# A hand-ordered beginning with raw weights ahead, in a two-layer kernel behind linear attention

## The chip, the cores and the metric

The kernel runs on one core of a Trainium2 chip. The metric is the device time of one execution in microseconds (us); lower is better. The engines are TensorE (PE, matrix multiplications), VectorE (DVE), ScalarE (ACT), GpSimd (POOL) and SyncE (SP, which here only starts transfers). Transfers (DMA) are started by an engine's queue and moved by 16 DMA engines.

## The reference

Linear attention on 8 batches of 8 heads, 576 tokens and head size 64, then two layers on the 4608 tokens of 512 features:

```python
kv  = np.einsum('bhsd,bhse->bhde', k, v)
out = np.einsum('bhsd,bhde->bhse', q, kv)
rms = np.sqrt(np.mean(out * out, axis=-1, keepdims=True) + 1e-06)
x   = (out / rms * g_norm)            # transposed to 4608 x 512
h   = x @ w_in;  x = (h * np.cos(h)) @ w_out        # 512 x 2048, 2048 x 512
a, b = x @ w1, x @ w2;  out = ((a * b) @ w3) @ w_out2
```

## The kernel before

All products are made in three matmuls: each fp32 operand is split in a rounded part (hi, ACT by line 113) and the rest (lo, DVE or POOL by line 115), and hi·hi, hi·lo and lo·hi are summed in PSUM (L532 to L534).

**Attention.** A unit u is half a batch (288 tokens); there are 16. Heads go in four pairs p. For a batch, `emit_kv` sums kᵀv of a pair (20 matmuls, L272) and `evac_kv` splits it; for a unit, `emit_qs` splits q, `emit_out` makes q·kv (3 matmuls, L313 to L315), `evac_out` squares it on ACT, `emit_ms` makes the mean squares (L332). Then comes the norm: `emit_rs` copies the mean squares (`ms_sb`) to DRAM and back in another shape (transfers `msd`, `rsx`), `emit_newton` finds the inverse root with 11 small DVE operations (L367 and L352 to L358), `emit_bc` sends it through DRAM once more (`rsd`) and spreads it over partitions (`bc`), `emit_x` multiplies, and `split_x` makes x in two parts. Units 2 and 3 use POOL's queue for all of these transfers (`queue`), the others SP's. Units 0 and 1 have a way of their own, `first_units`: their norm never leaves the chip (mean squares by L421, 11 operations of 96x48, spread over partitions by matmuls of L435).

**First layer.** A step n is a token block t of 512 tokens and a block m of 128 of the 2048 hidden features: `emit_h` (12 matmuls, h), `g_first` and `g_rest` (ACT and DVE: u, the cosine, then `u<-u,h` by L558, which also frees h's PSUM, and the split into g by L115), and two steps later `emit_w` (12 matmuls of g with w_out into x2). Steps 0 to 7 are t=0, m=0 to 7; steps 8 to 23 are t=1; then the rest. Token block 0 needs units 0 and 1, block 1 needs units 1 to 3.

**Weights.** w_in and w_out arrive as float64 words in 32 chunks of 512 KB (i0, i1 … of w_in, u0, u1 … of w_out), which `convert` turns into fp32 (one ACT operation and four on DVE, L142, L143, L146, L149) and `put` splits (ACT and DVE). Eight chunks are asked for, converted and put behind the first units ahead of step 0, the others among the steps.

**What sets the order.** The program is written in the order above, and the build's scheduler then places every instruction on its engine by a model of times of its own. The order is fixed when the program is built; on the chip an engine takes its instructions in that order and waits for what is not there yet. `issue_after(i)` holds what is written under it behind instruction i in that schedule. `marks[0]` is a small POOL operation (the gate) behind the second square of the third pair, and the loads of units 2 and 3 stand behind it. `quick` says at which step n which stage of units 2 and 3 is written.

Of the kernel before, what the change touches and what calls it, by code (L numbers as in the profile page):

```python
# [7 lines left out]
F32 = mybir.dt.float32  # L8
# [5 lines left out]
P = 128  # L14
# [15 lines left out]
def f32(ap):  # L30
    return ap.bitcast(F32)
# [3 lines left out]
def kernel(  # L35
# [75 lines left out]
    def split(dst, src, lo_engine=None):  # L111

        nc.scalar.activation(dst[:, 0], src, AF.Copy)  # L113
        lo_engine = lo_engine or even(src.shape[-1])
        lo_engine.tensor_tensor(dst[:, 1], src, f32(dst[:, 0]), ALU.subtract)  # L115
# [234 lines left out]
    def newton(x, y, t):  # L350

        nc.vector.tensor_scalar(  # L352
            y.bitcast(I32), x.bitcast(I32), -0.5, RSQRT_SEED, ALU.mult, ALU.add
        )
        for _ in range(3):
            nc.vector.tensor_tensor(t, x, y, ALU.mult)
            nc.vector.scalar_tensor_tensor(t, t, 0.5, y, ALU.mult, ALU.mult)
            nc.vector.scalar_tensor_tensor(y, t, 1.5, y, ALU.subtract, ALU.mult)  # L358
# [33 lines left out]
    def first_units(spread):  # L392

        for p in range(NPAIR):
            emit_kv(0, p)
            evac_kv(0, p)
            for u in range(2):
                if p == 0:
                    o_sb[u] = ap.tile([P, NPAIR, HALF], F32, tag="osb", bufs=3, name=f"o_{u}")
                hl = ap.tile([P, 2, HALF], F32R, tag="hl", bufs=2, name=f"qhl_{u}_{p}")  # L400
                split(hl, q_raw.pop((u, p)), nc.vector)
                ps = ps_acc.tile([P, 512], F32, tag=f"acc{(2 * p + u) % 4}", name=f"out_{u}_{p}")
                o, w = ps[:, 0:HALF], kv_sb[p]
                nc.tensor.matmul(o, w[:, 0], hl[:, 0], start=True, stop=False)
                nc.tensor.matmul(o, w[:, 1], hl[:, 0], start=False, stop=False)
                nc.tensor.matmul(o, w[:, 0], hl[:, 1], start=False, stop=True)
                sq = ap.tile([P, HALF], F32, tag="tmp", bufs=5, name=f"sq_{u}_{p}")
                nc.scalar.activation(sq, o, AF.Square)
                nc.scalar.activation(o_sb[u][:, p, :], o, AF.Identity, scale=gneg)
                if p == NPAIR - 2 and u == 1:  # L410
# [6 lines left out]
                if p == 0 and u == 0:  # L417
                    mst = ps_h.tile([P, 512], F32, tag="h", name="ms_first")
# [6 lines left out]
        n = 4 * NPAIR * NT3  # L425
        x, y, t = (row(f"rs_first_{i}")[0:T3, 0:n] for i in range(3))
        nc.vector.tensor_scalar(x, mst[0:T3, 0:n], EPS, HUGE, ALU.add, ALU.min)
        newton(x, y, t)
        for u in range(2):
            for p in range(NPAIR):  # L430
                ps = ps_acc.tile([P, 512], F32, tag=f"acc{p}", name=f"spread_{u}_{p}")
                for k in range(NT3):
                    at = ((u * NT3 + k) * NPAIR + p) * 2
                    for h in range(2):
                        nc.tensor.matmul(  # L435
                            ps[D * h:D * h + D, T3 * k:T3 * k + T3],
                            y[:, at + h:at + h + 1].to_broadcast([T3, D]), spread[0:T3],
                            start=k == 0, stop=True, skip_group_check=True,
                        )
                o = o_sb[u][:, p, :]  # L440
                nc.vector.tensor_tensor(o, o, ps[:, 0:HALF], ALU.mult)

    NEWTON, LAST = 8, 10
# [67 lines left out]

    def split_x(t, c, units=None):
# [8 lines left out]
        while done < TB:  # L521
            u, s = divmod(t * TB + done, HALF)
            w = min(TB - done, HALF - s)
            if units is None or u in units:
                split(
# [336 lines left out]
    if True:  # L862
# [8 lines left out]
        spread = wpool.tile([P, T3], F32, tag=f"wi{NM - 1}", name="spread")  # L871
# [4 lines left out]
        )  # L876

# [5 lines left out]
        load_kv(0, 0, "wi0")  # L883
        load_rest(0)
        for p in range(1, NPAIR):
            load_kv(0, p, f"wi{p}")
        for h in range(2):
            nc.sync.dma_start(
                out=gneg[D * h:D * h + D], in_=g_norm.rearrange("(d o) -> d o", o=1)
            )  # L890
        nc.vector.tensor_scalar(gneg, gneg, -1.0, None, ALU.mult)
        for p in range(NPAIR):
            for u in range(2):
                load_q(u, p, f"wi{4 + 2 * p + u}")
        first_units(spread)
        for c in range(KD):
            split_x(0, c)
        for _ in range(4):
# [22 lines left out]
        for n in range(NS + 2):  # L921
# [228 lines left out]
```

## Time and profile before

| | |
|---|---|
| runs before (us) | 1537.47, 1538.57, 1538.18; median 1538.18 |
| span of the profiled execution | 1537.0 us |
| the runs' median over that span | 1.2 us |
| PE busy | 1493.1 us, 97% of the span |
| DVE, ACT, POOL busy | 60%, 45%, 24% |
| granted PE clock in 40 slices of 38.4 us | 0.7 in the first, 0.9 or more in all others |

The page gives the profiled execution by its span alone, so that the sum of a change is made on the span of 1537.0 us and compared with the runs by the 1.2 us that their median stands above it. A row of the timeline reads: start in us, length in us, engine, line, operation, out<-in, shapes, count, and in brackets the idle time of the engine ahead of it with what ended that. The length of a matmul counts its way through the pipeline; matmuls that follow each other closely start 0.23 us apart at full clock and 0.43 us apart at half clock.

### The profile page before, as it was taken

What the parts mean: (1) busy time and instruction counts of PE and PEld (TensorE: products, weight loads), DVE (VectorE), ACT (ScalarE), POOL (GpSimd) and SP (SyncE); (2) the same over time, 40 slices, a digit from 0 to 9 for tenths busy, and PEclk for the clock granted to TensorE, in tenths of its full rate; (3) what the DMA queues carried; (4) which work ended last, traced back from release to release, by engine and by line L of the source; (5) the groups of instructions that cost most, each with busy time, mean ns of one, the idle gap of its engine ahead of it and who ended that gap; (6) DMA issues with size and microseconds to landing.
All of it is one profiled execution on the core that took longest, in us unless ns stands there. A gap on an engine that the chain in (4) does not pass through costs nothing.

```text
span 1537.0 us, 20537 instructions
## 1 busy us (share of the span) xinstructions
PE 1493.1 (97%) x7616; PEld 1272.3 (83%) x7616; DVE 924.6 (60%) x1714; ACT 696.8 (45%) x1405; POOL 368.5 (24%) x301
## 2 busy tenths in 40 slices
PE   6799999999999999999999998999999999999998
PEld 6577888788887787878888887999999998999997
DVE  4898855576566666766666447644543556545453
ACT  5667654444454454544534335433433334333331
POOL 1111010120010211101102007454444417344420
PEclk9799999999999999999999999999999999999999
DMA  8655120433333435234222015121202313223312
GB/s 300 207 156 165 42 72 7 150 110 113 112 105 98 137 98 155 86 109 133 89 78 96 1 48 185 42 83 69 69 28 82 110 64 108 84 88 123 124 62 76
DMA packets 81956, 156.26 MB, mean 102 GB/s; under 512 B 11600, under 2 KB 37376, under 8 KB 81856
## 3 DMA queue, kind: packets, MB, share of 16 engines
q1 hardware_dynamic: 80240, 150.18, 30.1%
q0 software_dynamic: 1616, 4.78, 1.1%
q8 instruction: 59, 0.97, 0.3%
q14 instruction: 41, 0.34, 0.1%
HBM read 113.77 MB, written 41.15 MB: 101 GB/s over the span
## 4 chain that ended last, share of the span: by engine, by line
PE 81%; DMA 6%; DVE 3%; POOL 2%; ACT 2%; issue 1%; SPq 0%; ACTq 0%; DVEq 0%; POOLq 0%
PE X L765 11%; PE h L532 8%; PE x L534 8%; PE x L533 8%; PE x L532 8%; PE h L533 8%; PE h L534 8%; PE V L765 5%; PE o L532 4%; PE o L533 4%; PE o L534 4%; PE Y L765 3%; POOL xc L115 2%; DMA x2r<-x_all 2%; PE kv L272 1%
## 5 line engine op out<-in xcount | busy, mean ns | idle before, releaser
L765 PE MATMUL X<-xc,w 128*128 128x384 f32 x1152 | 229.1, 337 | 6.7 <-ACT s L773 6.2
L534 PE MATMUL x<-g,w_out 128*128 128x512 f32 x576 | 225.6, 392 | 0.0
L533 PE MATMUL x<-g,w_out 128*128 128x512 f32 x576 | 225.2, 391 | 0.0
L532 PE MATMUL h<-x,w_in 128*128 128x512 f32 x544 | 216.1, 398 | 4.6 <-DVE u L558 2.9
L765 PEld LDWEIGHTS X<-xc,w 128*128 128x128 f32 x1152 | 203.6, 188 | 19.3 <-ACT s L773 10.2
L533 PE MATMUL h<-x,w_in 128*128 128x512 f32 x544 | 213.6, 393 | 1.8 <-DVE x L115 1.8
L532 PE MATMUL x<-g,w_out 128*128 128x512 f32 x576 | 212.4, 391 | 1.9 <-DVE x2s L579 1.1
L534 PE MATMUL h<-x,w_in 128*128 128x512 f32 x544 | 213.3, 392 | 0.0
L115 POOL TENSOR_TENSOR xc<-x2r,xc 128x768 fp32r<-128x768 f32 x70 | 133.0, 1907 | 226.2 <-ACT xc L113 226.2
L546 ACT ACTIVATE u<-h 128x512 f32<-128x512 f32 x144 | 86.1, 598 | 151.4 <-PE h L534 147.4
L557 ACT ACTIVATE u<-u 128x512 f32<-128x512 f32 x144 | 91.0, 632 | 121.7 <-DVE u L553 107.3
L115 DVE TENSOR_TENSOR g<-u,g 128x512 fp32r<-128x512 f32 x144 | 104.6, 727 | 64.0 <-ACT g L113 63.8
L113 ACT ACTIVATE g<-u 128x512 fp32r<-128x512 f32 x144 | 91.0, 632 | 108.4 <-DVE u L558 86.9
L115 POOL TENSOR_TENSOR qhl<-q,qhl 128x288 fp32r<-128x288 f32 x48 | 42.0, 878 | 393.6 <-ACT qhl L113 283.8
L532 PEld LDWEIGHTS h<-x,w_in 128*128 128x128 f32 x544 | 103.1, 190 | 30.5 <-DVE u L558 6.7
L532 PEld LDWEIGHTS x<-g,w_out 128*128 128x128 f32 x576 | 107.5, 188 | 24.6 <-DVE x2s L579 1.4
L533 PEld LDWEIGHTS x<-g,w_out 128*128 128x128 f32 x576 | 108.7, 189 | 22.9 <-DVE u_f L142 0.5
L534 PEld LDWEIGHTS x<-g,w_out 128*128 128x128 f32 x576 | 108.5, 188 | 22.8
L558 DVE TENSOR_TENSOR u<-u,h 128x512 f32<-128x512 f32 x144 | 98.6, 685 | 47.3 <-ACT u L557 46.9
L773 ACT ACTIVATE s<-X 128x384 f32<-128x384 f32 x144 | 65.9, 487 | 132.7 <-PE X L765 132.5
L552 DVE TENSOR_SCALAR r<-u 128x512 f32<-128x512 f32 x112 | 50.6, 452 | 122.1 <-ACT u L546 122.0
L533 PEld LDWEIGHTS h<-x,w_in 128*128 128x128 f32 x544 | 103.0, 189 | 23.0 <-DVE x L115 2.5
(183 smaller groups left out, 2646.5 us busy)
## 6 DMA issues: line engine op xcount, KB each, us to landing
x2r<-x_all SPq DMA_DIRECT2D x44, 384.0 KB
kvraw<-in_kv_main_dram SPq DMA_DIRECT2D x28, 512.0 KB
x_all<-x2s SPq DMA_DIRECT2D x36, 256.0 KB
part<-o SPq DMA_DIRECT2D x36, 256.0 KB
part<-part SPq DMA_DIRECT2D x36, 256.0 KB
out_dram<-part SPq DMA_DIRECT2D x36, 256.0 KB
i_w<-in_w1pair_dram SPq DMA_DIRECT2D x16, 512.0 KB
u_w<-in_w1pair_dram SPq DMA_DIRECT2D x16, 512.0 KB
```

The source lines that it names most:

```text
L113: nc.scalar.activation(dst[:, 0], src, AF.Copy)
L115: lo_engine.tensor_tensor(dst[:, 1], src, f32(dst[:, 0]), ALU.subtract)
L272: nc.tensor.matmul(ps[d, 0:D], k[:, d], v[:, d], start=i == 0, stop=i == NC)
L532: nc.tensor.matmul(ps, w[0], x[0], start=first, stop=False)
L533: nc.tensor.matmul(ps, w[0], x[1], start=False, stop=False)
L534: nc.tensor.matmul(ps, w[1], x[0], start=False, stop=last)
L546: nc.scalar.activation(u, h_ps[n], AF.Identity, bias=0.25, scale=INV_2PI)
L552: nc.vector.tensor_scalar(r, u, ROUND, ROUND, ALU.add, ALU.subtract)
L557: nc.scalar.activation(u, u, AF.Sin, scale=-TWO_PI_DOWN)
L558: nc.vector.tensor_tensor(u, u, h_ps.pop(n), ALU.mult)
L765: nc.tensor.matmul(ps, w[:, self.i, a, k], x[:, b, k], start=first and k == 0 and n == 0, stop=last and k == 1 and n == 2, skip_group_chec ...
L773: nc.scalar.activation(s, ps, AF.Copy)
```

## The change

It rewrites what comes ahead of step 0 and where units 2 and 3 begin:

- `load_first`: the raw words of chunk i0 are asked for ahead of k and v, those of i1 between the second and the third pair of k and v, i2 and the next behind the last. q of units 0 and 1 is one transfer for a pair; the first two pairs are started by ACT, the others by SP between the k, v loads. `g_norm` is loaded by POOL.
- `first_units` is split in stages (`kv`, `product`, `square`, `keep`, `scaled`) and, with `convert` and `put` of the first chunks among them, stands in `manual_schedule` for DVE and ACT: these two engines take the instructions in the order in which they are written, up to x of token block 0. The rounded part of q is made by DVE (a CAST, L437 of the new file) instead of ACT.
- Three chunks are converted or begun ahead of x, then three times two (before: four times two, behind `first_units` in the program).
- What is written from there until step 2 is closed stands behind the last operation of the Newton steps and the last spread matmul, and in steps 0 and 1 the stages of units 2 and 3 stand behind the last split of x as well.

```diff
+    def load_first():
+        ...
+        for t, src in pairs[:2]:
+            nc.scalar.dma_start(out=t, in_=src)
+        prefetch(1)
+        load_kv(0, 0, f"wi{NM - 2 * NPAIR}")
+        load_rest(0)
+        for p in range(1, NPAIR):
+            load_kv(0, p, f"wi{NM - 2 * NPAIR + p}")
+            if p == 1:
+                prefetch(2)
+            else:
+                t, src = pairs[p]
+                nc.sync.dma_start(out=t, in_=src)
+        prefetch(8)
...
+        kv(0)
+        product(0)
+        put(1)
+        square(0)
+        kv(1)
+        product(1)
+        keep(0)
+        convert(1)
+        square(1)
+        kv(2)
+        product(2)
+        keep(1)
+        put(1)
+        square(2)
+        kv(3)
+        product(3)
+        keep(2)
+        square(3)
+        convert(1)
+        nc.vector.tensor_scalar(x, mst[0:T3, 0:4 * NPAIR * NT3], EPS, HUGE, ALU.add, ALU.min)
+        newton_last = newton(x, y, t)
+        keep(3)
+        put(1)
+        scaled(0)
+        for p in range(1, NPAIR + 1):
+            if p < NPAIR:
+                scaled(p)
+            split_x(0, p - 1)
+        return newton_last.ins, spread_last[0].ins
...
-        first_units(spread)
-        for c in range(KD):
-            split_x(0, c)
-        for _ in range(4):
+        load_first()
+        behind = ExitStack()
+        with tc.manual_schedule(
+            engines={mybir.EngineType.DVE, mybir.EngineType.Activation}
+        ):
+            convert(1)
+            nc.vector.tensor_scalar(gneg, gneg, -1.0, None, ALU.mult)
+            last = first_units(
+                ...
+            )
+        x_first = list(x_last)
+        for i in last:
+            behind.enter_context(tc.issue_after(i))
+        for _ in range(3):
             prefetch(state["conv"] + 8)
             convert(2)
             put(2)
...
             for u, s in quick.get(n, ()):
                 one = [unit_stage(u, s)]
-                for i in range(4):
-                    run(one, i)
+                with ExitStack() as rest:
+                    for i in x_first if n < 2 else ():
+                        rest.enter_context(tc.issue_after(i))
+                    for i in range(4):
+                        run(one, i)
+            if n == 2:
+                behind.close()
```

The places that follow show what the build makes of it (a row: line, operation, out<-in with the names' numbers, partitions x columns). First SP's queue, from its start, before:

```order
L258 DMA kvraw_0_0_111<-in_kv_main_dram 128x1024
L247 DMA kvrest_0_113<-in_kv_tail_dram 128x512
L258 DMA kvraw_0_1_115<-in_kv_main_dram 128x1024
L258 DMA kvraw_0_2_117<-in_kv_main_dram 128x1024
L258 DMA kvraw_0_3_119<-in_kv_main_dram 128x1024
L888 DMA gneg_87<-in_g_norm_dram 64x1 x2
L297 DMA q_0_0_124<-in_qt_dram 128x288
```

and now:

```order
L133 DMA i0_w_119<-in_w1pair_dram 128x1024
L259 DMA kvraw_0_0_121<-in_kv_main_dram 128x1024
L248 DMA kvrest_0_123<-in_kv_tail_dram 128x512
L259 DMA kvraw_0_1_125<-in_kv_main_dram 128x1024
L133 DMA i1_w_127<-in_w1pair_dram 128x1024
L259 DMA kvraw_0_2_129<-in_kv_main_dram 128x1024
L413 DMA q_first_2_115<-in_qt_dram 128x2x288
```

The 1 MB of i0 and i1 stands ahead of the third pair of k and v, and q of the first pairs has left this queue. PE's line (not ordered by hand) has the third pair ahead of the end of the first product:

```order
L273 MATMUL kv_0_1_201<-kvraw_0_1_125 64x64 x8
L273 MATMUL kv_0_1_201<-kvrest_0_123 64x64 x2
L441 MATMUL out_0_0_177<-qhl_0_0_172,kv0_82 128x288
L442 MATMUL out_0_0_177<-qhl_0_0_172,kv0_82 128x288
L273 MATMUL kv_0_2_247<-kvraw_0_2_129 64x64 x8
L273 MATMUL kv_0_2_247<-kvrest_0_123 64x64 x2
L443 MATMUL out_0_0_177<-qhl_0_0_172,kv0_82 128x288
L441 MATMUL out_1_0_184<-qhl_1_0_173,kv0_82 128x288
```

Before, all four pairs stood ahead of the first product; now its third matmul waits for the third pair.

The second place is DVE where token block 0 ends and block 1 begins (step 7 to step 8). Before:

```order
L386 TENSOR_TENSOR o_3_782<-o_3_782,bc_3_1015 128x288 x4
L115 TENSOR_TENSOR g_6_1070<-u_6_1045,g_6_1070 128x512
L550 SCALAR_TENSOR_TENSOR u_7_1096<-r_7_1097,u_7_1096 128x512
...
L115 TENSOR_TENSOR x_1_1116<-o_3_782,x_1_1116 128x160 x4
...
L115 TENSOR_TENSOR g_7_1131<-u_7_1096,g_7_1131 128x512
...
L550 SCALAR_TENSOR_TENSOR u_8_1183<-r_8_1184,u_8_1183 128x512
...
L367 TENSOR_SCALAR rsx_4_1919<-rsx_4_1919 128x18
```

and now:

```order
L115 TENSOR_TENSOR g_7_1121<-u_7_1086,g_7_1121 128x512
L369 TENSOR_SCALAR rsx_3_933<-rsx_3_933 128x18
...
L388 TENSOR_TENSOR o_2_584<-o_2_584,bc_2_916 128x288 x4
...
L369 TENSOR_SCALAR rsx_4_1909<-rsx_4_1909 128x18
L388 TENSOR_TENSOR o_3_772<-o_3_772,bc_3_1005 128x288 x4
...
L115 TENSOR_TENSOR x_1_1106<-o_3_772,x_1_1106 128x160
...
L369 TENSOR_SCALAR rsx_5_2188<-rsx_5_2188 128x18
...
L625 SCALAR_TENSOR_TENSOR u_8_1173<-r_8_1174,u_8_1173 128x512
```

The norm of unit 3 begins behind g of step 7, where before x of block 1 was finished ahead of it; the norms of units 4 and 5 (`rsx_4`, `rsx_5`) stand ahead of u of step 8, where before the first of them stood well behind it.

The third place is PE at the same point. Before, the first matmul of step 8 stands ahead of most of step 6's `emit_w`, the products of unit 4 behind it:

```order
L272 MATMUL kv_2_3_1782<-kvrest_2_1489 64x64 x2
L532 MATMUL h_8_1170<-x_1_1116,w_in0_432 128x512
L533 MATMUL x2_0_0_727<-g_6_1070,w_out6_988 128x512
L534 MATMUL x2_0_0_727<-g_6_1070,w_out6_988 128x512
```

and now it stands behind step 7's `emit_w` and the products of units 4 and 5:

```order
L609 MATMUL x2_0_3_729<-g_7_1121,w_out7_1055 128x512
L314 MATMUL out_4_0_1656<-qhl_4_0_1594,kv0_82 128x288
...
L316 MATMUL out_5_3_2126<-qhl_5_3_2078,kv3_85 128x288
L333 MATMUL ms_5_2176<-sq_5_0_1962,sel_86 32x288
...
L607 MATMUL h_8_1160<-x_1_1106,w_in0_188 128x512
L607 MATMUL h_9_1199<-x_1_1106,w_in1_278 128x512
L333 MATMUL ms_5_2176<-sq_5_3_2139,sel_86 32x288
L608 MATMUL h_8_1160<-x_1_1106,w_in0_188 128x512
```

From `emit_w` of step 13 on PE's two orders are the same.

## Rows read from the trace of the kernel before

**Rows 1.** Windows: PE, PEld, DVE, ACT, POOL busy (instructions), PE clock, DMA share, GB/s.
```profile
60.00:70.00 10.00, 6.41 (x27) 3.21 (x25) 5.79 (x11) 8.27 (x19) 3.02 (x5) 0.83 0.59 187
70.00:80.00 10.00, 8.28 (x34) 5.89 (x35) 9.78 (x25) 6.38 (x13) 2.73 (x3) 0.65 0.48 128
...
110.00:120.00 10.00, 7.26 (x60) 5.22 (x59) 9.97 (x24) 9.39 (x27) 3.03 (x3) 0.89 0.56 138
```

**Rows 2.** Timeline of PE: first product, steps 2, 8, 10, 13.
```profile
13.41 0.68 PE L406 MATMUL out<-qhl,kv 128*128 128x288 f32 x2
...
71.72 0.80 PE L532 MATMUL h<-x,w_in 128*128 128x512 f32 x1 [2.23 <-DVE u L558]
77.07 0.67 PE L332 MATMUL ms<-sq,sel 128*32 128x288 f32 x2
78.17 0.73 PE L532 MATMUL x<-g,w_out 128*128 128x512 f32 x2
...
118.38 0.79 PE L532 MATMUL h<-x,w_in 128*128 128x512 f32 x1
...
132.85 0.51 PE L532 MATMUL h<-x,w_in 128*128 128x512 f32 x1 [0.21 <-DVE u L558]
...
164.09 0.39 PE L532 MATMUL h<-x,w_in 128*128 128x512 f32 x1
166.81 0.62 PE L532 MATMUL x<-g,w_out 128*128 128x512 f32 x2
```

**Rows 3.** Short windows in the beginning, same columns as rows 1.
```profile
10.00:11.00 1.00, 1.00 (x18) 0.77 (x15) 0.31 (x3) 0.22 (x1) 0.00 (x0) 1.00 1.01 352
18.00:19.00 1.00, 1.00 (x8) 1.00 (x7) 0.31 (x1) 1.00 (x4) 0.00 (x0) 1.00 1.02 414
22.00:24.00 2.00, 2.00 (x13) 2.00 (x13) 0.92 (x2) 1.24 (x4) 1.02 (x3) 1.00 1.02 416
```

**Rows 4.** Timeline of DVE: the first units' norm, single operations, end of x, first g.
```profile
27.22 0.20 DVE L427 TENSOR_SCALAR rs_first<-ms_first 96x48 f32<-96x48 f32 x1 [3.49 <-PE ms_first L421]
27.46 0.18 DVE L352 TENSOR_SCALAR rs_first<-rs_first 96x48 int32<-96x48 int32 x1
...
37.12 0.20 DVE L358 SCALAR_TENSOR_TENSOR rs_first<-rs_first,rs_first 96x48 f32<-96x48 f32 x1
...
47.71 0.42 DVE L142 TENSOR_SCALAR i_f<-i_f 128x512 f32<-128x512 f32 x1
48.05 0.69 DVE L115 TENSOR_TENSOR w_out<-u_f,w_out 128x512 fp32r<-128x512 f32 x1
48.65 0.69 DVE L149 SCALAR_TENSOR_TENSOR u_f<-u_w,u_f 128x512 int32<-128x512 int32 x1
49.25 0.45 DVE L115 TENSOR_TENSOR x<-o,x 128x288 fp32r<-128x288 f32 x1
49.62 0.45 DVE L441 TENSOR_TENSOR o<-o,spread 128x288 f32<-128x288 f32 x1
...
58.28 0.38 DVE L115 TENSOR_TENSOR x<-o,x 128x224 fp32r<-128x224 f32 x1
...
73.63 0.69 DVE L115 TENSOR_TENSOR g<-u,g 128x512 fp32r<-128x512 f32 x1
```

**Rows 5.** POOL's timeline: issues of unit 3's norm.
```profile
79.00 1.16 POOL L346 DMA_DIRECT2D msd<-ms_sb  x2 [4.00 <-ACT ms_sb L341]
...
82.86 0.56 POOL L347 DMA_DIRECT2D rsx<-msd  x1
```

**Rows 6.** The chain of waits: start, us, what (transfers of the norms).
```profile
67.99 2.20 DMA rsx<-msd
...
85.03 6.75 DMA bc<-rsd
...
107.62 2.02 DMA rsd<-rs
...
110.27 3.69 DMA bc<-rsd
```

More of the change, by code (lines that the diff above doesn't have):

```diff
@@ L390, with first_units, kv, product @@
     T3 = HALF // NT3
-    def first_units(spread):
+    def load_first():
+        pairs = []
         for p in range(NPAIR):
+            t = wpool.tile([P, 2, HALF], F32, tag=f"wi{NM - NPAIR + p}", name=f"q_first_{p}")
+            for u in range(2):
+                q_raw[u, p] = t[:, u]
+            pairs.append((t, qt[0, p].rearrange("u d s -> d u s")))
+        for t, src in pairs[:2]:
[11 more added lines that the diff above has]
+        prefetch(8)
+    def first_units(spread, x, y, t):
+        squares, hls = {}, {}
+        def kv(p):
             emit_kv(0, p)
             evac_kv(0, p)
+        def product(p):
+            if p % 2 == 0:
+                hl = [
+                    ap.tile([P, 2, HALF], F32R, tag="hl", bufs=2, name=f"qhl_{u}_{p}")
+                    for u in range(2)
+                ]
+            else:
+                both = ap.tile([P, 2, 2, HALF], F32R, tag="bc", name=f"qhl_{p}")
+                hl = [both[:, u] for u in range(2)]
             for u in range(2):
@@ L415, in first_units @@
                     )
-                if p == 0 and u == 0:
-                    mst = ps_h.tile([P, 512], F32, tag="h", name="ms_first")
                 for k in range(NT3):
@@ L424, in first_units, with keep, scaled @@
                     )
[L425 to L431, printed above, removed]
+        def keep(p):
+            for u in range(2):
+                nc.scalar.activation(
+                    o_sb[u][:, p, :], o_ps.pop((u, p)), AF.Identity, scale=gneg
+                )
+        def scaled(p):
+            for u in range(2):
+                ps = ps_acc.tile([P, 512], F32, tag=f"acc{(2 * p + u) % 4}", name=f"spread_{u}_{p}")
                 for k in range(NT3):
@@ L510, in load_halves @@
             halfway[name] += [t[:, k] for k in range(2)]
+    x_last = [None, None]
     def split_x(t, c, units=None):
@@ L524, in split_x @@
             if units is None or u in units:
-                split(
+                x_last[:] = split(
                     x_hl[t][:, :, c, done:done + w], o_sb[u][:, c, s:s + w],
@@ L876 @@
         )
+        for h in range(2):
+            nc.gpsimd.dma_start(
+                out=gneg[D * h:D * h + D], in_=g_norm.rearrange("(d o) -> d o", o=1)
+            )
         def run(stages, i):
@@ L881, in run @@
                     f()
[L883 to L889, printed above, removed]
-            )
[L891 to L894, printed above, removed]
-        first_units(spread)
-        for c in range(KD):
-            split_x(0, c)
-        for _ in range(4):
+        load_first()
[6 more added lines that the diff above has]
+            last = first_units(
+                spread,
+                *(firsts[0:T3, T3 + 48 * i:T3 + 48 * i + 48] for i in range(3)),
+            )
+        x_first = list(x_last)
+        for i in last:
+            behind.enter_context(tc.issue_after(i))
+        for _ in range(3):
             prefetch(state["conv"] + 8)
```

37 lines of the change are left out of this document (23 added, 14 removed).

## The prediction

> **What bounds the kernel now.** I read the windows first, because the change touches only the beginning: from `emit_w` of step 13 on PE's order is the same in both programs, and that matmul starts at 166.81 us [rows 2]. Whatever the change is worth is how much earlier or later this point is reached; behind it some 1370 us stay as they are. The windows [rows 1] show where the beginning is lax: PE is busy 6.41 of 10 us from 60 to 70, 8.28 from 70 to 80 at a mean clock of 0.65, and 7.26 from 110 to 120. The reader should see two holes: one ahead of the first `emit_w` (78.17), one ahead of step 8 (118.38). In the second DVE is busy for 9.97 us; in the first it idles in 60 to 70 (5.79 busy).
>
> PE's timeline [rows 2] gives the marks. The first products end at 14.09 (13.41 and 0.68). Step 2's h waits for DVE (`u L558`, which frees its PSUM) until 71.72 and takes 5.35 us, half speed, up to the mean squares at 77.07. Steps 8 and 10 begin at 118.38 and 132.85. DVE's timeline [rows 4] gives the same from its side: the first norm from 27.22 to 37.32, x of block 0 finished at 58.66, g of step 0 at 74.32. The chain of waits [rows 6] shows the DRAM round trips of a norm: 2.20 us for `rsx`, 2.02 for `rsd`, 3.69 to 6.75 for `bc`.
>
> **A, the loads.** Ahead of the third pair of k, v the queues now hold 3392 KB: i0 and i1 (1024), three pairs of k, v (1536), the rest (256), q of two pairs (576). In the beginning the DMA moves 352 GB/s [rows 3], later 414. 3.47 MB at 352 is 9.9 us; 2.3 to 3.3 us for the first issue and the last landing are my estimate, which no row here shows; that gives 12.2 to 13.2. PE's order puts this pair (1.5 us) ahead of the last matmul of the first product, so that the first pair's two outputs end near 15.9, not at 14.09: 1.8 later. The other end: if ACT's queue adds bandwidth, the 576 KB fall out and it is 1.7 earlier.
>
> SP alone moved 414 GB/s from 18 to 19, SP and POOL together 416 from 22 to 24 [rows 3]: a second queue brought nothing, so I don't take the other end. The Trainium skill ("DMA: Bandwidth & Descriptors", section "Issuing engines are not separate DMA queues") says the same as a rule against this part of the change: transfers of all issuing engines share 16 DMA engines, and a second issuer saves only issue time. By that rule the q transfers only compete.
>
> From there to the norm PE, DVE and ACT take the pairs in turn. Before it was 13.1 us (14.09 to 27.22) for three pairs and the mean squares. Now q's rounding has moved from ACT to DVE, eight CASTs. None is in the trace; the nearest rows are a one-input operation of 128x512 at 0.34 us from one start to the next (47.71 to 48.05) and a two-input one of 128x288 at 0.37 (49.25 to 49.62). I take 0.27 each, bounds 0.2 and 0.46. Two casts a pair and the conversions on DVE's line make a pair 3.75 to 4.75 us; with 4.3 and a last 1.9 for mean squares the norm's input is complete at 30.8. The four operations of i2's conversion stand directly ahead of the norm; they overlap with PE's tail except 1.0. The eleven norm operations are back to back now: 27.22 to 27.46 is 0.24 each, 2.6 in all. The norm ends at 34.4 instead of 37.32, **2.9 earlier**.
>
> The Trainium skill ("VectorE: DVE Perf Modes", section "Mode 2×_2P") lets a one-source copy from SBUF deliver two elements a cycle, which two-source operations cannot. By it, scaled from the 0.34 row, a cast would be near 0.2 and the norm 0.5 us earlier.
>
> **B, x of block 0.** DVE then has 43 operations: 16 of 128x512 with two inputs at 0.60 (48.05 to 48.65), 11 with one at 0.34, 12 of 128x288 at 0.37, 4 of 128x224 at 0.30: 19.0 us [rows 4]. x ends at 53.4 instead of 58.66: **5.3 earlier**, since units 2 and 3 stand behind it.
>
> **C, to the first `emit_w`.** The next 25 operations come to 10.0 by the same prices and 10.4 with gaps; g of step 0 ends at 63.8 instead of 74.32. `u<-u,h` of step 0 ends at 60.7 and frees step 2's PSUM; this h takes 5.35 at half speed as before, then 1.2 for products of unit 2: T = 67.2, against 78.17: **11.0 earlier** (13.7 at full clock). But before, at 78.17, all eight products of units 2 and 3 and most of their mean squares were done. Now five products (0.40 each) and the mean squares (1.3) are owed: 3.3 us of PE.
>
> **D, to the mean squares of unit 3.** 121 main matmuls at 2.72 per twelve (164.09 to 166.81 [rows 2]) are 27.4, with what is owed 31: M = 98.2. DVE needs some 39.7, by the prices of B, from g of step 0 to g of step 7 (to 103.5); so neither waits long.
>
> **E, the change of token block.** Here a wait takes the place of the one removed. Unit 3's norm begins only now. Before, from the end of unit 3's mean squares at 77.74 to the issue of `msd` (79.00), of `rsx` (82.86) [rows 5] and its landing 2.2 later it took 7.4 to 7.9; so DVE has `rsx_3` at M+7.5. The 26 DVE rows of this norm, with conversions and unit 2's x among them, take 7.9, and up to 2 for unit 2's `bc`: norm at N = M+16.4 = 114.6. From there to landed `bc` it is 6.6 (107.32 to 113.96 [rows 6]), then scale and split: step 8's first h near N+8.5 = 123. PE has done step 7's `emit_w` and the products of unit 5 by N+1.5 or so and idles some 7, then restarts at half clock. The last mean square of unit 5 stands among step 8's matmuls (N+10.5), and on DVE the norms of units 4 and 5 stand ahead of u of step 8: another 7.4 for `rsx_5`, so N+17.6, and 4 for the norm, u and `u<-u,h`. Step 10's h waits for this: N+22 = **136.6, against 132.85**. PE idles 5 more here.
>
> **F, to step 13.** Before, 33.96 us lay between step 10's h and `emit_w` of 13. Eleven halves of a step at 2.72 remain, 29.9, since the products and mean squares that were mixed in are done: 166.5, and 1.8 for a clock that restarts low. I get 168.3 against 166.81.
>
> **Sum.** 11.0 won by T, 3.3 owed, 7 and 5 of new idle time, 1.8 of clock, against 4.6 us of waits and half-speed matmuls that the program before had from 110 to 140 and that go (2.7 of them are the idle time in 110 to 120 [rows 1]): 1.5 later. Span 1538.5; the runs' median lies 1.2 above the span shown, so **1539.7**. A measurement of this kernel tells 0.2%, 3.1 us, from no change, so this is no change. The own range of this case is 1536.5 to 1543: the clock at step 2 (2.7), the casts (0.5 to 1) and the landings.
>
> **The rivals.**
>
> *Faster: the hand-over hides.* If unit 3's norm is ready as PE ends step 7, because T comes later on PE than on DVE or the norm's transfers find an empty queue, the two idle times shrink from 12 to 3 us. For it: the DMA share is 0.5 to 0.6 from 70 to 120 [rows 1], and 11 us of lead stand. Against it: DVE's order has `rsx_3` behind g of step 7. It gives 1539.7 less 9, 1530.7. It decides if unit 3's mean squares are done 7 us before 98.
>
> *Slower: the norms of units 4 and 5 hold u of step 8.* The mechanism is the DVE line, where `rsx_5` stands ahead of u. Its transfers share SP's queue with weights and q; with a `bc` of 6.75 instead of 3.69 [rows 6] for unit 3 and a q of unit 5 as late, step 10's h comes 3 to 6 later, 140 to 143. It gives 1543 to 1546; it decides as soon as `rsx_5` lands after 133.
>
> *The beginning isn't earlier.* If the loads bound it (i0, i1 and q ahead of k, v), pairs at 4.75 put the norm at 36 and T at 69: part of the lead is gone, 1541.5. If, at the other end, the second queue adds bandwidth, 1538.
>
> **How the numbers follow.** The forecast, with the variants of the beginning, gets 0.40; the faster rival 0.28; the slower 0.32, because the wait is in the program's order, while its size rests on transfers of varying length. Range 1530 to 1546: both rivals' times with 0.1 left out at either end. Chances: faster 0.28, same 0.40, slower 0.32.
>
> **What would show it.** Right: norm of the first units near 34, x complete near 53, first `emit_w` near 67, then PE idle time of 5 us or more ahead of step 8 and again ahead of step 10, with `rsx` as releaser of DVE there; `emit_w` of step 13 at 165 to 171. Wrong: a first norm after 36 (A), a first `emit_w` after 70 (C), or step 8 starting right behind step 7 without idle time (E). Rows behind step 13 that moved against each other by more than 1 us would break the ground of the whole sum.

## The result: slower, by a chain that starts late

| | before | changed |
|---|---|---|
| median of 4 runs each (us) | 1537.84 (1537.47 to 1538.57) | 1548.51 (1547.73 to 1549.39) |
| ratio, 95% interval | 1 | 1.0062 [1.0047, 1.0078] |
| span of the profiled execution (us) | 1537.0 | 1546.8 |

The change costs 9.8 us in the profiled spans, all of it ahead of `emit_w` of step 13: this starts at 176.93 instead of 166.81 [rows 2], and from there to the end it is 1369.9 us after and 1370.2 before. The marks, each the start or the end (start plus length) of a row in the timelines; where no word says which, a start:

| mark (us) | before | predicted | after |
|---|---|---|---|
| norm of the first units ends (DVE) | 37.32 | 34.4 | 34.89 |
| x of block 0 complete (DVE) | 58.66 | 53.4 | 53.82 |
| g of step 0 ends (DVE) | 74.32 | 63.8 | 65.99 |
| first `emit_w` starts (PE) | 78.17 | 67.2 | 69.44 |
| last mean squares of unit 3 end (PE) | 77.74 | 98.2 | 102.27 |
| DVE has `rsx_3` | 85.85 | 105.7 | 109.98 |
| norm of unit 3 ends (DVE) | 107.32 | 114.6 | 121.18 |
| step 8's first h (PE) | 118.38 | 123 | 133.01 |
| step 10's first h (PE) | 132.85 | 136.6 | 144.36 |
| `emit_w` of step 13 (PE) | 166.81 | 168.3 | 176.93 |

The page of the changed kernel, span and engines:

```profile
span 1546.8 us, 20510 instructions
PE 1499.3 (97%) x7616; PEld 1276.2 (83%) x7616; DVE 926.7 (60%) x1722; ACT 694.1 (45%) x1397; POOL 368.5 (24%) x303
```

A loss of 10 us hides in these shares; the windows show it (columns as in rows 1; first the answers to [rows 1], then the next ten):

```profile
60.00:70.00 10.00, 7.74 (x41) 5.86 (x42) 9.84 (x21) 8.17 (x19) 1.09 (x2) 0.66 0.54 178
70.00:80.00 10.00, 10.00 (x49) 7.75 (x48) 9.72 (x21) 8.24 (x18) 0.55 (x1) 1.00 0.69 236
110.00:120.00 10.00, 6.38 (x72) 4.92 (x68) 8.58 (x26) 5.83 (x17) 2.56 (x2) 0.95 1.03 316
120.00:130.00 10.00, 6.36 (x23) 3.80 (x23) 1.04 (x6) 4.99 (x14) 4.14 (x6) 0.67 0.59 164
```

The first hole has shrunk: from 70 to 80 PE is now busy throughout at full clock, against 8.28 us at 0.65. The second has grown. From 120 to 130 DVE, busy for 8.58 us in the ten before, works 1.04 of 10 us: it waits for a transfer, and PE, at a clock of 0.67, waits too. PE's timeline:

```profile
62.81 0.80 PE L607 MATMUL h<-x,w_in 128*128 128x512 f32 x1 [2.26 <-DVE u L633]
69.44 0.40 PE L607 MATMUL x<-g,w_out 128*128 128x512 f32 x1
...
101.60 0.67 PE L333 MATMUL ms<-sq,sel 128*32 128x288 f32 x2
...
126.74 0.40 PE L314 MATMUL out<-qhl,kv 128*128 128x288 f32 x1 [1.22 <-ACT qhl L113]
...
130.24 0.61 PE L314 MATMUL out<-qhl,kv 128*128 128x288 f32 x1 [2.09 <-ACT qhl L113]
...
131.90 1.18 PE L333 MATMUL ms<-sq,sel 128*32 128x288 f32 x6
133.01 1.22 PE L607 MATMUL h<-x,w_in 128*128 128x512 f32 x2
...
144.36 0.80 PE L607 MATMUL h<-x,w_in 128*128 128x512 f32 x1 [3.47 <-DVE u L633]
...
176.93 0.39 PE L607 MATMUL x<-g,w_out 128*128 128x512 f32 x1
```

These answer to [rows 2]. What is new stands between 126 and 133: products of unit 5 that wait for their q ahead of step 8. DVE, against [rows 4]:

```profile
34.69 0.20 DVE L359 SCALAR_TENSOR_TENSOR rs_first<-rs_first 96x48 f32<-96x48 f32 x1
...
53.44 0.38 DVE L115 TENSOR_TENSOR x<-o,x 128x224 fp32r<-128x224 f32 x1
...
65.30 0.69 DVE L115 TENSOR_TENSOR g<-u,g 128x512 fp32r<-128x512 f32 x1
...
109.98 0.16 DVE L369 TENSOR_SCALAR rsx<-rsx 128x18 f32<-128x18 f32 x1
...
121.00 0.18 DVE L359 SCALAR_TENSOR_TENSOR rs<-rs,rs 128x18 f32<-128x18 f32 x1
130.71 0.38 DVE L369 TENSOR_SCALAR rsx<-rsx 128x18 f32<-128x18 f32 x1 [9.54 <-DMA rsx<-msd]
131.01 1.55 DVE L388 TENSOR_TENSOR o<-o,bc 128x288 f32<-128x288 f32 x4
...
140.22 0.18 DVE L369 TENSOR_SCALAR rsx<-rsx 128x18 f32<-128x18 f32 x1 [4.03 <-DMA rsx<-msd]
```

The norm of unit 3 ends at 121.18. The next instruction on DVE is the start of unit 4's norm, and it waits 9.54 us for its transfer, with the scaling of unit 3 (`o<-o,bc`) queued behind it. At 140.22 the same happens with unit 5, and u of step 8 waits. POOL's issues for unit 3 (to [rows 5]) and the chain of waits of the profile (to [rows 6]):

```profile
103.80 1.17 POOL L347 DMA_DIRECT2D msd<-ms_sb  x2 [3.35 <-ACT ms_sb L342]
106.64 1.00 POOL L348 DMA_DIRECT2D rsx<-msd  x1 [1.08 <-issue]
...
121.47 0.58 POOL L378 DMA_DIRECT2D rsd<-rs  x1 [2.84 <-DMA q<-in_qt_dram]
124.21 1.24 POOL L382 DMA_DIRECT2D bc<-rsd  x2
```

```profile
125.56 4.11 DMA q<-in_qt_dram
129.75 0.45 ACT qhl L113
...
131.97 1.11 PE ms L333 x6
133.08 1.15 PE h L607 x2
```

Two lines end at step 8 here. The chain of waits goes through the second: a q of unit 5 lands, its products and mean squares follow on PE, and step 8's h stands right behind them. The first part of x, which comes by way of the scaling on DVE (131.01), is ready some 1 us before that.

### The profile page after: what moved, and what is told of

Its sections match the earlier page's. It is cut to its first block, busy times and chain, and to the rows that moved or that the text cites. A ratio compares the mean times of both kernels' runs of the same rounds, so it can differ in the third digit from the quotient of the medians.

```text
span 1546.8 us, 20510 instructions
## 1 busy us (share of the span) xinstructions
PE 1499.3 (97%) x7616; PEld 1276.2 (83%) x7616; DVE 926.7 (60%) x1722; ACT 694.1 (45%) x1397; POOL 368.5 (24%) x303
## 4 chain that ended last, share of the span: by engine, by line
PE 85%; DMA 5%; DVE 3%; POOL 2%; ACT 2%; issue 1%; SPq 1%; ACTq 0%; DVEq 0%
PE X L840 11%; PE h L607 9%; PE h L608 8%; PE h L609 8%; PE x L607 8%; PE x L609 8%; PE x L608 8%; PE V L840 5%; PE o L607 4%; PE o L608 4%; PE o L609 4%; PE Y L840 3%; POOL xc L115 2%; DMA x2r<-x_all 2%; PE kv L273 2%
```

## The experiments

Two theories. **The lead is lost by the order** (theory A in the expectations): the hold lets block 0 begin earlier, but ties the norm of units 2 and 3 to the same point, and that chain is longer than the work PE has left; what else stands on DVE's line (conversions) decides when both begin. **Single waits at the change of block** (theory C for the first of them): the norms of units 4 and 5 on DVE's line, transfers under load, or the latency of Newton's steps cost the 10 us and can be taken out by themselves. A third, that the new loading order or queue is at fault (theory B), was tried too.

What is given as measured is the median in us, then the ratio to the kernel before with its 95% interval. The ratio is taken against executions of the kernel before on the same chip; those have medians from 1536.86 to 1537.84 us.

### The hold: undone, and done alone

`e1_free`, the change without its two holds:

```diff
-        for i in last:
-            behind.enter_context(tc.issue_after(i))
...
-                    for i in x_first if n < 2 else ():
+                    for i in ():
```

> The changed kernel with units 2 and 3 let go again: neither held behind the first norm and spread nor behind the last split of x; the loads and the hand-made order up to x stay. Theory A (the loss is the held second batch: unit 3's norm ended at 121.2 instead of 107.3 us, and PE idles behind it from 112 to 145): unit 3's norm ends at 100 to 108, step 8 begins at or ahead of 118, the time falls by 12 to 17 us below the changed kernel, to 1531 to 1537. Theory B (the loads cost it: raw weights and q ahead of k, v, later transfers that collide): the time stays within 4 us of the changed kernel. Theory C (only the place of the norms of units 4 and 5 on VectorE's line costs it): it falls by some 6 to 10, since that place moves with it.

Measured: 1540.28, 1.0024 [1.0015, 1.0033]. DVE's and PE's timelines:

```profile
51.76 0.20 DVE L359 SCALAR_TENSOR_TENSOR rs_first<-rs_first 96x48 f32<-96x48 f32 x1
```
```profile
83.50 0.73 PE L607 MATMUL x<-g,w_out 128*128 128x512 f32 x2
...
118.37 0.40 PE L607 MATMUL h<-x,w_in 128*128 128x512 f32 x1
...
170.22 1.07 PE L607 MATMUL x<-g,w_out 128*128 128x512 f32 x4
```

Step 8 is back where it was before the change (118.37 against 118.38), but the first norm ends at 51.96, since units 2 and 3 and conversions are now laid among its operations. The holds bring both the lead and the loss. The time fell by 8.2 us, less than theory A asked for; 6 to 10 is the price of theory C, which `e3_hold45` below tests.

`e8_before_held`, the kernel before with the hold on x alone:

```diff
+        x_first = list(x_last)
...
-                for i in range(4):
-                    run(one, i)
+                with ExitStack() as rest:
+                    for i in x_first if n < 2 else ():
+                        rest.enter_context(tc.issue_after(i))
+                    for i in range(4):
+                        run(one, i)
```

> The kernel before with one part of the change alone: in steps 0 and 1 the stages of units 2 and 3 are held behind the last split of x of block 0. Its beginning has no lead to lose. Theory A: unit 3's norm ends 12 to 18 us later than in the kernel before and the time rises by 10 to 18 us above before, to 1548 to 1556. Theory B: within 3 us of before. Theory C: 3 to 6 above before, since rsx of unit 4 stands among the splits of x of block 1 here too.

Measured: 1547.32, 1.0059 [1.0042, 1.0075]; its runs lie from 1541.17 to 1548.2, and the profiled one is the fastest. PE:

```profile
67.55 0.63 PE L535 MATMUL x<-g,w_out 128*128 128x512 f32 x2
...
128.82 0.63 PE L535 MATMUL h<-x,w_in 128*128 128x512 f32 x1
```

With nothing of the new beginning, the same lead (first `emit_w` at 67.55) and the same loss: the intervals overlap with the change's. So the beginning is not what costs. Nor does it bring the lead: the first norm ends at 33.92 here.

### Parts of the beginning

`e12_plain`: the change without the raw weights ahead, the second queue and the conversions among the first units; order by hand and holds stay.

> The changed kernel without raw weights ahead of k, v, q all on SP behind k, v as before, and no conversion among the first units (four times two behind them as before); the hand-made order and both holds stay. If the lead at the first emit_w comes from the hold alone, as the run of before with the hold suggests (67.6 us there, 69.4 in the changed kernel), this is within 2 us of the changed kernel and its first emit_w at 66 to 71. If raw weights ahead bring the lead, the first emit_w comes at 73 or later and the time is 4 us or more above the changed kernel.

Measured: 1550.91, 1.0088 [1.0066, 1.0109]; first `emit_w` 71.78, step 8 135.50. The first norm ends at 33.15, 1.7 earlier than in the change, and the first `emit_w` comes 2.3 later; the intervals overlap. No gain from the raw weights ahead or from the second queue shows in the time.

`e5_spq`: all of q on SP's queue (`nc.scalar.dma_start` to `nc.sync.dma_start` for the first two pairs).

> The changed kernel with all of q started by SP, the first two pairs ahead of i0. If a second queue only saves issue time, the first product ends within 0.7 us of 16.5 and the time is within 2 us of the changed kernel; if ACT's queue had added bandwidth, k and v land 1.5 us or more later than in the changed kernel.

Measured: 1550.82, 1.0081 [1.0062, 1.0101]. The first pair of k and v is ready at 10.00 instead of 8.02, because i0 is issued 1.0 us later, behind q's two issues, and 0.6 MB of q goes ahead. The first products end 1.2 earlier (15.23 against 16.46), the first norm 1.5 later (36.4). The marks named in the expectation went against "only issue time", but they don't tell bandwidth from order, since q has changed its place too. The transfers from 2 to 8 us do, the change first:

```profile
DMA packets 888, 1.75 MB, mean 291 GB/s; under 512 B 91, under 2 KB 535, under 8 KB 888
DMA packets 885, 1.70 MB, mean 283 GB/s; under 512 B 84, under 2 KB 581, under 8 KB 885
```

Two queues moved 1.75 MB there, one 1.70: the second is worth order and issue time, as A had it, and the interval of the time overlaps with the change's.

`e4_loads`: the old order of loads under the new hand order.

> The changed kernel with the transfers in the order of the kernel before: k, v first, then q of all pairs on SP, then the raw weights; the hand-made order and the holds stay. Theory A: the first norm ends within 2 us of 34.9 and step 8 waits as before; time within 3 us of the changed kernel. Theory B: 6 us or more below the changed kernel. Theory C: as A.

Measured: 1557.62, 1.0126 [1.0110, 1.0142]; first norm 41.25, first `emit_w` 75.19. This one decides little: DVE's and ACT's hand order begins with i0's conversion, so a later i0 holds everything.

### The norms of units 4 and 5, and Newton's latency

`e3_hold45`, where `rsx_4` may not stand ahead of unit 3's scaling:

```diff
+            def held():
+                with tc.issue_after(x_block1[0]) if u in (4, 5) else nullcontext():
+                    emit_newton(u)
-            late.append(lambda: emit_newton(u))
+            late.append(held)
```

> The changed kernel with the Newton steps of units 4 and 5 held behind the last split of x of block 1; units 2 and 3 stay held as in the change. Theory A: the idle time ahead of step 8 stays (unit 3's norm still ends near 121), so the first h of step 8 comes at 130 or so instead of 133.0; the wait for rsx_5 ahead of u of step 8 goes (3.5 us of PE) or moves behind it; time 3 to 6 us below the changed kernel, still 4 or more above before. Theory B: within 2 us of the changed kernel. Theory C: all 10 us come back, about the time of before.

Measured: 1545.09, 1.0059 [1.0043, 1.0075]. DVE:

```profile
128.73 2.16 DVE L388 TENSOR_TENSOR o<-o,bc 128x288 f32<-128x288 f32 x4 [8.28 <-DMA bc<-rsd]
...
133.21 0.17 DVE L369 TENSOR_SCALAR rsx<-rsx 128x18 f32<-128x18 f32 x1
```

PE:

```profile
131.41 1.18 PE L333 MATMUL ms<-sq,sel 128*32 128x288 f32 x6
132.52 0.80 PE L611 MATMUL h<-x,w_in 128*128 128x512 f32 x1
```

The 9.54 us under `rsx` become 8.28 under `bc`: behind the wait that was taken away stood another of nearly its length, the norm's way through DRAM (`rsd`, `bc`). The scaling begins 2.3 us earlier than in the change, but step 8 at 132.52 only 0.5, and the norm had ended 0.7 earlier already. What stands ahead of step 8 is PE's line: the mean squares of unit 5 end there without idle time, behind products that wait for a q (landed at 128.84, chain of waits). So neither `rsx_4` nor `bc` alone sets step 8; the q of unit 5 was a third line of nearly the same length, and no run takes it away by itself. The intervals overlap; the medians differ by 3.4 us, the ratios by 0.5.

`p1_after_pool`, `p2_before_pool` and `p3_paced_pool` move nine of the eleven Newton operations of units 2 and 3 to POOL, where they are written as twelve (in the change, in the kernel before, in `f4_fewer_first` below), so that the norm doesn't queue behind DVE's conversions:

```diff
+            nc.gpsimd.tensor_tensor(t, x, y, ALU.mult)
+            nc.gpsimd.tensor_tensor(t, t, y, ALU.mult)
+            nc.gpsimd.tensor_scalar(t, t, 0.5, 1.5, ALU.mult, ALU.subtract)
+            nc.gpsimd.tensor_tensor(y, t, y, ALU.mult)
```

> [...] If the stretch of the norm on VectorE's line is the link that costs, unit 3's norm ends 4 to 8 us earlier than 121.2, step 8 begins at 124 to 129 instead of 133, and the time falls by 4 to 9 us. If q and products of unit 5 on TensorE's line hold step 8 in any case, the norm ends earlier and step 8 moves by less than 2 us.

> The kernel before with the same move. Unit 3's norm (85.9 to 107.3 there) ends at 90 to 96, but VectorE was full from 110 to 120, so step 8 begins only 1 to 5 us earlier than 118.4; time 0 to 4 us below before.

> The paced version (the fastest so far, 1534.6) with the same move. Its norm of unit 3 took from 95.0 to 108.1 and bc landed at 120.6; with both norms ended 5 to 10 us earlier step 8 begins at 110 to 117 instead of 121.5: 1527 to 1533. If products of units 4 and 5 hold step 8, within 1.5 us of the paced version.

Measured: 1551.84, 1.0084 [1.0064, 1.0105]; 1544.01, 1.0039 [1.0026, 1.0052]; 1534.99, 0.9982 [0.9970, 0.9993]. In the first the norm of unit 3 takes 7.3 us from `rsx_3` to its end (114.80 to 122.1) instead of 11.2, but `rsx_3` comes 4.8 later, and step 8 begins at 135.01. In the third step 8 begins 3.8 earlier than in `f4_fewer_first` (117.67) and `emit_w` of step 13 3.2 earlier (162.26 against 165.42), but from there to the end it takes 1372.5 instead of 1367.6. No gain in time anywhere: a misfire.

### The conversions on DVE's line

`f1_paced_only` keeps both holds and all of the beginning. Behind the three chunks among the first units, two instead of six are converted ahead of step 0, then two a step up to 18 chunks (by step 8 the change has 21) and one a step from there:

```diff
-        for _ in range(3):
+        for _ in range(1):
...
-            more = min(n_first, 9 + n + min(n, 8) // 2) - state["conv"] if n < NS else 0
+            more = min(n_first, (min(2 * n + 5, 18) if n <= 8 else n + 10)) - state["conv"] if n < NS else 0
```

> The paced version with both holds of the change and without the held norms of units 4 and 5. On VectorE's line rsx of unit 4 stands ahead of unit 3's scaling again. If that place matters here as in the changed kernel, 2 to 6 us above the paced version, 1536.5 to 1541; if not, within 1.5 us of it.

Measured: **1534.85, 0.9981 [0.9968, 0.9995]**, 13.7 below the change and the best version with `f4_fewer_first`. PE and DVE:

```profile
56.15 1.09 PE L607 MATMUL x<-g,w_out 128*128 128x512 f32 x4
...
82.22 0.67 PE L333 MATMUL ms<-sq,sel 128*32 128x288 f32 x2 [0.60 <-ACT sq L324]
...
119.58 0.79 PE L607 MATMUL h<-x,w_in 128*128 128x512 f32 x1 [0.46 <-ACT x L113]
...
130.80 0.80 PE L607 MATMUL h<-x,w_in 128*128 128x512 f32 x1 [3.87 <-DVE u L633]
...
163.47 0.39 PE L607 MATMUL x<-g,w_out 128*128 128x512 f32 x1
```
```profile
93.21 0.18 DVE L369 TENSOR_SCALAR rsx<-rsx 128x18 f32<-128x18 f32 x1
...
106.60 0.18 DVE L359 SCALAR_TENSOR_TENSOR rs<-rs,rs 128x18 f32<-128x18 f32 x1
...
118.70 1.57 DVE L388 TENSOR_TENSOR o<-o,bc 128x288 f32<-128x288 f32 x4 [0.56 <-DMA bc<-rsd]
```

The first `emit_w` starts 13.3 us earlier than in the change, the norm of unit 3 ends 14.4 earlier, step 8 starts 13.4 and `emit_w` of step 13 13.5 earlier. What was taken off DVE's line ahead of step 0 arrives undiminished. Four chunks less are ahead of step 0. At the spacings of [rows 4], 0.34 with one input and 0.60 with two, a chunk costs DVE 2 × 0.34 + 2 × 0.60 for its conversion and 0.60 for its split: 2.5 us, and 10 of the 13.3 us for four.

The others of this kind, by edit. `f4_fewer_first`: the same with the norms of 4 and 5 held as in `e3_hold45` and the hold on x left out. `f1c_paced`: `range(2)` and `2 * n + 7`. `k1_before_held_paced`: the kernel before with the hold of `e8_before_held`, two of its four pairs of chunks and `2 * n + 5`. `f2b_before_paced`: the kernel before without hold, three pairs, `2 * n + 6`. `g1_after_gentle` and `g2_before_gentle`: the change and the kernel before with only `n + 10` behind step 8. `e9_late` and `e10_before_late`: both with the conversions beyond 18 put off to two a step from step 13 on, `max(min(9 + n + min(n, 8) // 2, 18), 2 * n - 7)`.

> The changed kernel with its hold behind the first norm, but with the conversions paced by need: two chunks instead of six behind the first units, then two a step up to the 18 that steps 0 to 9 need, the others one a step from step 9 on; the Newton steps of units 4 and 5 held behind x of block 1 and the second hold (behind the last split of x) left out. It keeps the early beginning and lets unit 3's norm come earlier on VectorE's line (row 175 instead of 205). Theory A (step 8 waits for unit 3's norm, which is late because the second batch stands behind other VectorE work): first emit_w at 62 to 69, norm of unit 3 at 104 to 113 instead of 121, step 8 at 116 to 125 instead of 133; time 8 to 16 us below the changed kernel, 1532 to 1540. If the norm comes earlier and step 8 does not, theory A falls and products and q of units 4 and 5 ahead of step 8 on TensorE's line are what it waits for.

> The changed kernel with both holds and the conversions paced between it and the other (four chunks behind the first units). Theory A: a smaller dose of the same: unit 3's norm 4 to 8 us earlier than 121, time 3 to 8 us below the changed kernel.

> The kernel before with the hold behind the last split of x and the paced conversions, and with nothing else of the change: loads, queues, GpSimd's gate and the scheduler's own order of the first units as before. If hold and pacing are all that counts, within 3 us of the paced changed kernel (1534.9). If the new beginning itself is worth its difference at the first emit_w, 4 us or more above it.

> The kernel before with the conversions paced by need (six chunks behind the first units instead of eight, then as in the runs above), nothing held. First emit_w some 4 us earlier than 78.2; step 8 at 112 to 120. Within 4 us of before either way; if this is as fast as the paced changed kernel, the pacing alone and not the new beginning is worth having.

> The changed kernel with only the conversions that no step ahead of 16 needs written later (18 chunks by step 8 instead of 21, one a step from there). The mean squares of unit 3 stay at 102 us, since nothing ahead of them moves. If unit 3's mean squares set the rest, the time falls by at most 5 us below the changed kernel (steps 8 to 10 are a little earlier); if the later conversions are what counts, it falls by 10 or more.

> The kernel before with only the conversions that no step ahead of 16 needs written three steps later (18 chunks by step 8 instead of 21), one a step behind that. In the run with a steeper pace the later steps lost what step 8 to 13 had won (step 20's h at 193.6 instead of 191.3). If that loss came from the steep pace, this is 1 to 4 us faster than before; if VectorE has no room there in any case, the same as before.

> The changed kernel, with the conversions that no step ahead of step 16 needs (i10, u8, i11 and later) written in steps 13 and on instead of 6 to 12; same sums. Theory A1 (the change of token block waits for the chain of unit 3's norm: mean squares at 102.2, DRAM round trips, norm at 121.2): only VectorE's part of that chain shrinks, 2 to 5 us of the 19 from mean squares to norm; the time falls by 2 to 6 us below the changed kernel and stays above before. Theory A2 (VectorE's work as such, full from 35 to 113 us, is what step 8 waits for): three conversions of 2.5 us ahead of step 8 go, the time falls by 7 or more. A loss is possible where the conversions collide with steps 13 to 18.

> The kernel before with the same late conversions, as a control. In it unit 3's scaling waits for VectorE more than for transfers (99.7% busy from 110 to 120). Theory A1: 1 to 4 us faster than before, since step 8 begins at 112 to 117. Theory A2: 4 to 7 us faster.

| kernel | median, ratio [95%] | first `emit_w` | step 8 | between |
|---|---|---|---|---|
| *with hold* | | | | |
| the change | 1548.51, 1.0062 [1.0047, 1.0078] | 69.44 | 133.01 | 63.6 |
| `e8_before_held` | 1547.32, 1.0059 [1.0042, 1.0075] | 67.55 | 128.82 | 61.3 |
| `f1_paced_only` | 1534.85, 0.9981 [0.9968, 0.9995] | 56.15 | 119.58 | 63.4 |
| `f4_fewer_first` | 1534.62, 0.9980 [0.9970, 0.9991] | 56.52 | 121.50 | 65.0 |
| `f1c_paced` | 1542.13, 1.0032 [1.0022, 1.0043] | 66.00 | 122.68 | 56.7 |
| `k1_before_held_paced` | 1543.34, 1.0038 [1.0020, 1.0056] | 63.69 | 129.34 | 65.7 |
| `g1_after_gentle` | 1544.15, 1.0055 [1.0034, 1.0076] | 68.80 | 128.26 | 59.5 |
| `e9_late` | 1552.16, 1.0083 [1.0062, 1.0104] | 68.75 | 129.01 | 60.3 |
| *without* | | | | |
| before | 1537.84 | 78.17 | 118.38 | 40.2 |
| `e1_free` | 1540.28, 1.0024 [1.0015, 1.0033] | 83.50 | 118.37 | 34.9 |
| `f2b_before_paced` | 1546.45, 1.0053 [1.0033, 1.0073] | 71.00 | 128.12 | 57.1 |
| `g2_before_gentle` | 1538.33, 1.0004 [0.9991, 1.0017] | 76.75 | 116.98 | 40.2 |
| `e10_before_late` | 1542.21, 1.0021 [1.0006, 1.0037] | 77.17 | 118.16 | 41.0 |

Read the last column. With a hold (one of the two or both) step 8 trails the first `emit_w` by 57 to 66 us in these kernels (61 to 69 in `e3_hold45`, `e12_plain`, `e5_spq`, `e4_loads`, `p1_after_pool` and `p3_paced_pool`), whatever the beginning; in the kernel before it is 40, because units 2 and 3 are done with their products by then. So with the hold the lead counts only if the first `emit_w` comes early enough. From step 8 to `emit_w` of step 13 it is 48.4 us before and 43.9 both after and in `f1_paced_only`, since more is done ahead; step 8 may come 4.5 us later than 118.4 and break even. 122.9 less 63.5 is 59.4: the change's 69.44 lies 10.0 above, `f1_paced_only` 3.3 below, and the times are 10.7 and −2.7 against before. The rule is rough: `f1c_paced` has step 8 at 122.68 and is yet 5 us slower than before. At step 13 it is 1.2 behind (167.98); the rest comes later. From that mark to the end the profiled executions take between 1366.8 and 1372.7 us (more in `e9_late` and `e10_before_late`, which put work there), so a gain of 3 us at the change of block need not be seen in the time.

The hold is not the only way to a late step 8. `f2b_before_paced` has none, and its mean squares of unit 3 are copied at 80.01 (78.31 before); but on DVE's line the norm stands among conversions and ends at 117.27 instead of 107.32, and step 8 comes 57 us behind the first `emit_w`. Any edit lets the scheduler lay the whole order anew, and this one moved the norm.

`k1_before_held_paced` and `f1_paced_only` have the hold on x and the pace alike and differ by the new beginning with its second hold: 1543.34 against 1534.85, 8.5 us. What the beginning saves is real, once the line behind it is short. Fewer conversions ahead are no gain by themselves: the same pace brings 13.7 us in the changed kernel, 4.0 in the kernel before with the hold (`k1_before_held_paced` against `e8_before_held`, with overlapping intervals), and in the kernel before without it `f2b_before_paced` is a miss, 9 us slower. `e10_before_late` reaches `emit_w` of step 13 2.5 earlier than before (164.32) and loses 6.4 behind it, where the conversions now stand; `e9_late` gains 4.2 and loses 3.3 in the same way, and its interval overlaps with the change's. `g1_after_gentle` has a median 4.4 below the change's, but the intervals overlap; `g2_before_gentle` gained nothing.

## Why the prediction was wrong

The time is 8.8 us above the forecast and 2.5 above the upper end of its range. `emit_w` of step 13 came 8.6 later than forecast: 2.2 of that arose in C, 1.8 in D, 3.7 in E (5.9 ahead of step 8, less 2.2 behind it) and 0.9 in F.

**The ground of the sum** held: rows behind step 13 moved by 0.3 us.

**A (loads, first norm)** held within 0.5 us. The third pair of k and v had landed at 13.68, past the 12.2 to 13.2 of the estimate, and the first products ended 0.6 later than the 15.9. The choice against a wider second queue was right, as `e5_spq` shows; but one row was misread. From 22 to 24 us all packets were SP's (queue q1), so that the 416 GB/s are no sum of two queues:

```profile
q1 hardware_dynamic: 228, 0.83, 102.3%
```

From 24 to 26, where both queues moved data, it was 387 GB/s, which bears the choice out. The casts took more than the 0.27 taken:

```profile
11.26 0.31 DVE L437 CAST qhl<-q_first 128x288 fp32r<-128x288 f32 x1
11.61 0.46 DVE L438 TENSOR_TENSOR qhl<-q_first,qhl 128x288 fp32r<-128x288 f32 x1
```

A cast and the operation behind it start 0.35 apart; eight times 0.08 is 0.6, about what the norm was late, but that the casts made it late is not shown: ahead of i2's conversion, right before the norm, DVE idled 1.81 us for ACT. The estimate of 0.2 by the Trainium skill ("VectorE: DVE Perf Modes", section "Mode 2×_2P") did worse than the row: the one-source cast is 1.5 times as fast here as the two-source row below it (0.31 against 0.46), not twice. Its rule of two elements a cycle agrees with what a column more costs: with 0.42 and 0.69 for 128x512 [rows 4], 224 columns more are 0.11 us with one source and 0.23 with two. The scaling from 128x512 failed because a part of each operation does not shrink with its columns.

**B (x of block 0)** held to 0.4 us. **C (first `emit_w`)** was 2.2 too early; step 2's h was released at 62.81 instead of 60.7, and 1.7 of that arose on DVE's line behind x. **D (mean squares)** came 1.8 further behind than priced (102.27 against 98.2, of which 2.2 came from C).

**E (change of block) is the step that failed.** From the mean squares of unit 3 to step 8 it took 30.7 us; E priced 24.8. Its parts: to the end of the norm 18.9 instead of 16.4, nearly all of it on DVE's line behind `rsx_3` (11.2 against 8.9); from there to step 8 11.8 instead of 8.5. The second E had put at 6.6 for the way of `bc` and 1.9 for scale and split, as if nothing stood ahead of them. The kernel before itself had taken 11.1 over this stretch (107.32 to 118.38): E took the landing of `bc` at 113.96 from it and left out the 2.1 us until DVE came to the scaling:

```profile
116.09 1.55 DVE L386 TENSOR_TENSOR o<-o,bc 128x288 f32<-128x288 f32 x4
```

In the change the scaling began 9.8 us behind the norm (131.01 less 121.18) and the rest took 2.0. Of the 9.8 the transfers alone explain 8.3, by `e3_hold45`; `rsx_4`, which the order shown ahead of the prediction has ahead of `o_3`, holds the scaling for the rest. E had priced that order for step 10 only. On PE's line E had the products of unit 5 done 1.5 us behind the norm; they ended 10.8 behind it (131.97), because their q was issued at 125.56, behind transfers for unit 4 on SP's queue, and took 4.11 us to land. From step 8 to step 10 E was too dear (11.35 instead of 13.5), and **F** came within 1 us (32.6 against 31.7).

The kind of the mistake is size. That the lead would be paid back at the change of block was in the sum: by D and E step 8 trails the first `emit_w` by 55.8 us, against 40.2 before. It was 63.6. So the lead of 8.7 us was bought with 23.4 us more, of which the work done ahead gives back 4.5 behind step 8: a tie became a loss of 10. The hold by itself, in `e8_before_held`, has the same balance.

**The slower rival** named two things that are there (norms of units 4 and 5 on DVE ahead of what step 8 needs, transfers late), and its condition came true: `rsx_5` at 140.22, past its 133. But it put the loss between step 8 and step 10, and there the change was faster than forecast; `rsx_5` was late because step 8 was. Its price, 1543 to 1546, was too low by 2.5, as it built on E. In `e3_hold45`, with `rsx_4` and `rsx_5` out of the way, most of the loss stays. **The faster rival** fell by its own condition: unit 3's mean squares were 4 us later than 98, not 7 earlier. **The beginning isn't earlier** fell.

Open: which of the lines that end at step 8 (`rsx_4`, `bc`, the q of unit 5) sets it once the others are gone, and how much of the 30.7 us is transfers under load. Neither holding the norms of 4 and 5 nor moving Newton's operations shortened them by much, and nothing was run that takes the transfers of q and weights out of the stretch from 110 to 120.

## What to carry to other kernels

Before work is held back so that other work starts sooner, lay out its whole chain to the point where its result is needed, DRAM round trips included, and set it against the work that the busy engine has left; a lead that is shorter than that is paid back. Work done ahead of need on an engine that is full (here four chunks of conversions) can be as dear as late work: in the changed kernel postponing it was worth more than the whole new beginning, in the kernel before it was not, since the order came out otherwise. When one wait is taken away, look for the one that stands behind it, on every engine's line.

## What the runs showed of the hardware that was not expected

The 128x18 operations that mostly take 0.16 to 0.18 us on DVE take 0.23 to 0.74 on POOL, twelve of them 5.7 us:

```profile
116.45 0.60 POOL L368 TENSOR_TENSOR rs<-rsx,rs 128x18 f32<-128x18 f32 x1 [6.50 <-DVE rs L364]
...
119.77 0.74 POOL L370 TENSOR_SCALAR rs<-rs 128x18 f32<-128x18 f32 x1
...
121.91 0.23 POOL L371 TENSOR_TENSOR rs<-rs,rs 128x18 f32<-128x18 f32 x1
...
127.30 1.27 POOL L393 DMA_DIRECT2D bc<-rsd  x2 [4.25 <-DMA rsd<-rs]
```

That is the timeline of POOL in `p1_after_pool`, for unit 3. Behind the norm `bc` could not be issued for another 4.25 us, until `rsd` had landed.
